# High-by-high matmuls first in steps 0 and 1, the second tile's scores in four quadrants, the first third in a new order

## The chip, the cores and the metric

The kernel runs on one core of a Trainium2 chip. Its time is the device time of one execution in microseconds (us); lower is better. Five engines work in parallel, each through its own list of instructions in order: PE (TensorE, matmuls), ACT (ScalarE), DVE (VectorE), POOL (GpSimd) and SP (SyncE, which here issues most transfers).

## The reference

Attention in chunks of 64 tokens, then a feed-forward layer with g = h·cos(h):

```
scores = scale * q_c @ k_c^T        # batch 8, heads 8, 9 chunks of 64, head size 64
attn   = softmax(scores); out = attn @ v_c
x = out as 4608 tokens x 512
h = x @ w_in                        # 512 x 2048
g = h * cos(h)
result = g @ w_out                  # 2048 x 512
```

The inputs are float32, or arrive as 8-byte words that the kernel turns into float32 itself (here they do, for the weights).

## The kernel before, in words

The 4608 tokens are nine tiles of 512. For a tile, a pair of heads (hp 0 to 3) is one 128x512 array: its scores are 16 matmuls of 64x64 on PE, DVE takes each chunk row's maximum from them and subtracts it, ACT takes the exponential, DVE sums and inverts, DVE or POOL divides, PE transposes (tiles 0 and 1) into a tile `pts`, and PE multiplies with the values. The result x is needed as two parts: `x_hi` (a rounding cast by ACT) and `x_lo` (the remainder, by DVE). Every weight is treated the same way: ACT decodes two halves of its words, DVE joins them, ACT or DVE casts `w_hi`, DVE or POOL makes `w_lo`. A product of two such operands is three matmuls: high by high, high by low, low by high.

The feed-forward layer runs in steps s; a step takes one block of 128 of the 2048 columns. `hidden` (L701) makes h for the step: 12 matmuls of 128x512, three for each of four column blocks cc of x (cc is the head pair hp). Then comes a chain of six: ACT (turn count), DVE, ACT (sine), DVE (the product g), a cast `g_hi` and a remainder `g_lo`. `project` (L735) multiplies with w_out: three matmuls for each of four banks `acc`, 12 in a step, three steps behind. Two banks `h` are in turns, so that `hidden` of step s waits until step s-2 has its g.

The program builds its work as a list of pieces (`piece`, L1079): an engine, an estimated length, a function that records the instructions, and the pieces that it waits for. Which piece comes when on which engine is read from two tables, `RANK` and `ELSEWHERE` (L91 on), whose numbers were made ahead; `in_order` (L282) only sorts by them. What each engine runs is then fixed.

Tile 0's and tile 1's attention is in `early` (L1144). In both, a head pair's scores fill one bank: head 0's into partitions 0 to 63, head 1's into 64 to 127 (`scores_early`, L489), so that the 16 matmuls alternate between two quadrants of the array (rows of head 0 with columns of head 0, rows of head 1 with columns of head 1). Tile 1's four head pairs use the banks a0 and a1 in turns. From tile 2 on, `scores` (L522) makes two head pairs at once into both banks, one bank for each head, and a bank's upper and lower partitions take the even and odd chunks: four quadrants in turn, 64 matmuls in the trace's count for two head pairs (a matmul of float32 there counts twice). Steps 0 and 1 (s < `BY_HEAD`, L1287) record their hidden matmuls in four pieces each, one for each cc with its three matmuls; a piece waits for all of the weight's split, w_lo included (`split`), and both halves of its x, x_lo included (`x_done`).

Of the kernel before, what the change touches and what calls it, by code (L numbers as in the profile page):

```python
# [288 lines left out]
def attention_then_cos_ffn(ctx: ExitStack, tc, qT, kT, v, w_in, w_out, out, wide):  # L289
# [232 lines left out]
    def scores(t, g, banks):  # L522
# [3 lines left out]
        for j in range(2):  # L526
            qt, kt = queries.pop((t, 2 * g + j))
            for c in range(NCH):
                pr, par = divmod(c, 2)
                cs, ps = slice(c * CH, (c + 1) * CH), slice(par * CH, (par + 1) * CH)  # L530
                o = (j * NPR + pr) * CH
                for h in range(2):
                    hs = slice(h * CH, (h + 1) * CH)

# [1964 lines left out]
```

## Time and profile before

| what | us |
|---|---|
| median of three runs | 775.62 |
| lowest and highest of the three | 774.85 and 776.1 |
| span of the profiled execution, first to last instruction | 773.5 |
| PE busy in it | 762.5 (99%) |
| DVE busy in it | 644.4 (83%) |
| ACT busy in it | 444.8 (58%) |

No other time of the profiled execution is given than its span. An engine's busy share is its busy time by the span. PE is busy nearly always, so what counts is where it still waits, and how many matmuls it has to run; in the rows on PE, matmuls overlap, and the start of a row to the start of the next says what a row costs.

### The profile page before, as it was taken

To read this page: it belongs to the slowest core of one execution; us is meant where nothing else is said; L and a number is where in the kernel's file an instruction comes from. 1 tells how busy PE (TensorE), PEld (TensorE's weight loads), DVE (VectorE), ACT (ScalarE), POOL (GpSimd) and SP (SyncE) were. 2 spreads that over 40 slices of the span, in tenths; PEclk is the share of its full clock that TensorE was granted. 3 is DMA by queue.
4 is the path that set the end of the run, shared out by engine and by line. 5 is a ranking of instruction groups with operands and counts; after the bars stand their busy time and mean duration, and the time that the engine had idled before them with its cause. 6 is when DMAs were issued, how large, how long until landed. Compare 5 with 4: busy or idle time off the path is not lost.

```text
span 773.5 us, 16085 instructions
## 1 busy us (share of the span) xinstructions
PE 762.5 (99%) x6100; PEld 676.3 (87%) x6100; DVE 644.4 (83%) x1112; ACT 444.8 (58%) x818; POOL 267.1 (35%) x245
## 2 busy tenths in 40 slices
PE   7999999999999999999999999999999999999997
PEld 6888888888999988888888888888888888989997
DVE  5998989989899889897898868785998577798874
ACT  5999876456874456554553435546554355557651
POOL 3422133776542444246222321200202315265231
PEclk9999999999999999999999999999999999999999
DMA  9995600579979753777974545587535567988983
GB/s 341 401 410 197 205 2 1 190 263 382 320 255 310 243 165 108 226 259 243 326 265 140 174 135 188 181 290 242 179 104 180 158 208 229 294 300 284 361 305 103
DMA packets 95757, 177.22 MB, mean 229 GB/s; under 512 B 9152, under 2 KB 39872, under 8 KB 95680
## 3 DMA queue, kind: packets, MB, share of 16 engines
q1 hardware_dynamic: 95104, 175.15, 66.2%
q8 instruction: 48, 0.79, 0.4%
q10 hardware_dynamic: 576, 1.05, 0.4%
q14 instruction: 29, 0.24, 0.1%
HBM read 127.93 MB, written 48.23 MB: 228 GB/s over the span
## 4 chain that ended last, share of the span: by engine, by line
PE 84%; DVE 8%; DMA 4%; ACT 2%; issue 1%; SPq 0%; DVEq 0%; ACTq 0%
PE acc L323 39%; PE h L323 33%; PE a L323 12%; DMA w_in<-sums 2%; DMA sums<-qt 1%; DMA combo<-w_in 1%; DVE w_in L970 1%; DMA kt<-in_kT_dram 1%; DVE z L595 0%; DVE w_in L344 0%; DVE pts L640 0%; DVE w_in L937 0%; DVE g L724 0%; DVE m L546 0%; DVE g L726 0%
## 5 line engine op out<-in xcount | busy, mean ns | idle before, releaser
L323 PE MATMUL acc<-w_out,g_hi 128*128 128x512 f32 (+1 forms) x976 | 278.1, 369 | 0.0
L323 PE MATMUL h<-x,w_in 128*128 128x512 f32 (+1 forms) x960 | 226.4, 364 | 0.1
L323 PEld LDWEIGHTS acc<-w_out,g_hi 128*128 128x128 f32 x976 | 178.5, 189 | 22.9
L323 PEld LDWEIGHTS h<-x,w_in 128*128 128x128 f32 x960 | 171.1, 189 | 22.7 <-ACT g_hi L340 0.4
L323 PE MATMUL acc<-w_out,g_lo 128*128 128x512 f32 (+1 forms) x488 | 179.2, 367 | 0.0
L344 POOL TENSOR_TENSOR g_lo<-g,g_hi 128x512 fp32r<-128x512 f32 x30 | 41.4, 1380 | 194.3 <-ACT g_hi L340 70.9
L323 PEld LDWEIGHTS acc<-w_out,g_lo 128*128 128x128 f32 x488 | 92.4, 189 | 11.8 <-DVE g_lo L344 0.2
L323 PE MATMUL h<-w_in,w_in 128*128 128x512 f32 (+1 forms) x384 | 98.3, 354 | 0.8 <-DVE w_in L970 0.7
L323 PEld LDWEIGHTS h<-w_in,w_in 128*128 128x128 f32 x384 | 65.6, 190 | 9.7 <-DVE w_in L970 2.0
L980 ACT ACTIVATE w_in<-w_in 128x512 f32<-128x512 f32 x64 | 39.3, 628 | 17.8 <-DVE w_in L976 17.7
L344 DVE TENSOR_TENSOR g_lo<-g,g_hi 128x512 fp32r<-128x512 f32 x59 | 44.1, 747 | 4.0 <-ACT g_hi L340 2.2
L340 ACT CAST g_hi<-g 128x512 fp32r<-128x512 f32 x48 | 29.7, 618 | 27.8 <-PE acc L323 14.5
L323 PE MATMUL a<-w_in,w_in 128*128 128x512 f32 (+1 forms) x204 | 42.5, 348 | 0.0
L323 PE MATMUL a<-x,w_in 128*128 128x512 f32 (+1 forms) x192 | 41.2, 353 | 0.0
L344 POOL TENSOR_TENSOR g_lo<-w_in,g_hi 128x512 fp32r<-128x512 f32 x12 | 18.9, 1577 | 64.3 <-ACT g_hi L340 42.6
L323 PEld LDWEIGHTS a<-w_in,w_in 128*128 128x128 f32 x204 | 34.5, 190 | 4.0
L323 PEld LDWEIGHTS a<-x,w_in 128*128 128x128 f32 x192 | 33.2, 190 | 4.1
L967 ACT COPY a<-h 128x512 f32<-128x512 f32 x28 | 16.0, 571 | 32.3 <-PE h L323 32.1
L723 ACT ACTIVATE g<-h 128x512 int32<-128x512 f32 x32 | 19.3, 602 | 26.1 <-PE h L323 26.0
L973 ACT ACTIVATE w_in<-h 128x512 int32<-128x512 f32 x32 | 19.1, 597 | 26.3 <-PE h L323 24.7
L976 DVE SCALAR_TENSOR_TENSOR w_in<-w_in,h 128x512 f32<-128x512 int32 x32 | 21.9, 685 | 12.6 <-ACT w_in L973 11.8
L344 DVE TENSOR_TENSOR g_lo<-w_in,g_hi 128x512 fp32r<-128x512 f32 x34 | 28.8, 855 | 3.8 <-ACT g_hi L340 3.2
(294 smaller groups left out, 1509.6 us busy)
## 6 DMA issues: line engine op xcount, KB each, us to landing
w_in<-combo SPq DMA_DIRECT2D x84, 512.0 KB, 4.8
combo<-w_in SPq DMA_DIRECT2D x56, 256.0 KB, 4.5
w_in<-combo SPq DMA_DIRECT2D x56, 256.0 KB, 5.3
qt<-in_qT_dram SPq DMA_DIRECT2D x36, 256.0 KB, 5.6
w_in<-in_w_in_dram SPq DMA_DIRECT2D x16, 512.0 KB, 9.7
kt<-in_kT_dram SPq DMA_DIRECT2D x32, 256.0 KB, 5.6
w_out<-in_w_out_dram SPq DMA_DIRECT2D x16, 512.0 KB, 9.9
gathered<-w_in SPq DMA_DIRECT2D x32, 256.0 KB, 3.7
```

What stands on the lines that cost most here:

```text
L323: kept(nc.tensor.matmul(*args, **kw))
L340: kept(nc.scalar.copy(out=out, in_=in_))
L344: kept(eng.tensor_tensor(out, a, b, op=op))
L723: lambda: kept(nc.scalar.activation(n, h, AF.Identity, bias=0.25, scale=0.5 / math.pi)),
L967: kept(nc.scalar.copy(out=out, in_=in_))
L970: kept(nc.vector.tensor_tensor(out, a, b, op=ALU.add))
L973: kept(nc.scalar.activation(g.bitcast(I32), h, AF.Identity, bias=0.25, scale=0.5 / math.pi))
L976: kept(nc.vector.scalar_tensor_tensor(g, g.bitcast(I32), -2.0 * math.pi, h, op0=ALU.mult, op1=ALU.add))
L980: kept(nc.scalar.activation(g, g, AF.Sin, bias=0.5 * math.pi))
```

## The change

Four things change.

1. In steps 0 and 1, `hidden` records the four high-by-high matmuls as pieces of their own, which need only `w_hi` and `x_hi`. The two with a low part form a second piece for each cc.
2. Tile 1's scores are made by `scores`, two head pairs at once into banks a0 and a1, in four quadrants. A chunk c = 2 pr + par of tile 1 goes to the partitions of pr mod 2, so that chunks 0 and 1 lie in the lower half, 2 and 3 in the upper. Four pieces for scores become two. The weights' layout and the transposed tile's column index follow.
3. `RANK` and `ELSEWHERE` hold new numbers, which change the order in the first third of the work. Behind some 1,220 of PE's 3,158 rows the order is the same as before.
4. With the order, single operations change engine: the copies of transposed tiles and some casts from ACT to DVE, some remainders to POOL.

```diff
@@ scores @@
-                cs, ps = slice(c * CH, (c + 1) * CH), slice(par * CH, (par + 1) * CH)
-                o = (j * NPR + pr) * CH
+                row, at = (pr % 2, pr - pr % 2 + par) if t == 1 else (par, pr)
+                cs, ps = slice(c * CH, (c + 1) * CH), slice(row * CH, (row + 1) * CH)
+                o = (j * NPR + at) * CH
...
-        e = weights_of(t, g).rearrange("p a (r h) k -> p a r h k", h=2)
+        e = weights_of(t, g).rearrange("p a (h r) k -> p a r h k" if t == 1 else "p a (r h) k -> p a r h k", h=2)
@@ weighted @@
+                        at = 4 * h + pr if t == 1 else 2 * pr + h
                         matmul(
-                            banks[par][hs, o : o + CH], vt[ks, fs], pts[ks, fs],
+                            banks[par][hs, o : o + CH], vt[ks, fs], pts[ks, at * CH : (at + 1) * CH],
@@ hidden @@
-    def hidden(t, fc, ccs=range(4), h=None):
+    def hidden(t, fc, ccs=range(4), h=None, highs=True, lows=True):
...
-            matmul(h, w_hi[:, ws], x_hi, start=(cc == 0), stop=False)
+            if not lows:
+                matmul(h, w_hi[:, ws], x_hi, start=(cc == 0), stop=False)
+                continue
+            if highs:
+                matmul(h, w_hi[:, ws], x_hi, start=(cc == 0), stop=False)
             matmul(h, w_hi[:, ws], x_lo, start=False, stop=False)
             matmul(h, w_lo[:, ws], x_hi, start=False, stop=(cc == NCC - 1))
@@ early @@
-        for hp in range(HP):
-            which = ("a", hp % 2) if t else ("acc", hp)
+        for g in range(2) if t else ():
+            key = ("s", t, g)
+            now = piece(
+                PE, 1.1, made_by(key, lambda g=g: scores(t, g, (bank("a", 0), bank("a", 1)))),
+                banks_free.get(("a", 0)), banks_free.get(("a", 1)), at=max(here["qk", t, 2 * g + j] for j in range(2)),
+                lag=0.35, pairs=64,
+            )
+            below = []
+            for h in range(2):
+                m = piece(DVE, 0.6, rest_of(key, 2 * h), now)
+                below.append(piece(DVE, 0.6, rest_of(key, 2 * h + 1), m, turned_out.get((t - 1, g))))
+                banks_free["a", h] = below[-1]
...
@@ steps 0 and 1 @@
         if s < BY_HEAD:
-            for cc in range(NCC):
-                def go(t=t, fc=fc, key=key, cc=cc):
-                    made[key] = hidden(t, fc, (cc,), made.get(key))
-                stream = piece(
-                    PE, 0.648, go, stream if cc else begun, split["in", fc], bank_at, *x_done[t][2 * cc : 2 * cc + 2],
-                    pairs=3, main=True,
-                )
-                begun = begun if cc else stream
+            for lows in (False, True):
+                for cc in range(NCC):
+                    def go(t=t, fc=fc, key=key, cc=cc, lows=lows):
+                        made[key] = hidden(t, fc, (cc,), made.get(key), not lows, lows)
+                    stream = piece(
+                        PE, 0.432 if lows else 0.216, go, stream if cc or lows else begun,
+                        split["in", fc] if lows else high_of["in", fc], bank_at,
+                        *(x_done if lows else x_high)[t][2 * cc : 2 * cc + 2], pairs=2 if lows else 1, main=True,
+                    )
+                    begun = begun if cc or lows else stream
```

The order on PE around the end of steps 0 and 1, before. Names: `w_in_479` and `w_in_525` are the split weights of steps 0 and 1, `w_in_569` of step 2; `x_0` and `x_2` are the high parts of tile 0's x for cc 0 and 1 and for cc 2 and 3, `x_1` and `x_3` the low parts; `a<-kt,qt` are tile 1's scores, a row of 16 for one head pair (its first head pair's stands far ahead, among tile 0's transposes).

```order
L323 MATMUL h<-x_2_516,w_in_479 128x512
L323 MATMUL h<-x_0_442,w_in_525 128x512
L323 MATMUL h<-x_1_443,w_in_525 128x512
L323 MATMUL h<-x_0_442,w_in_525 128x512
L323 MATMUL a_584<-kt,qt 64x64 x16
L323 MATMUL h<-x_2_516,w_in_525 128x512
L323 MATMUL h<-x_3_517,w_in_525 128x512
L323 MATMUL h<-x_2_516,w_in_525 128x512 x2
L323 MATMUL h<-x_3_517,w_in_525 128x512
L323 MATMUL h<-x_2_516,w_in_525 128x512
L323 MATMUL a_618<-kt,qt 64x64 x16
L323 MATMUL a_642<-kt,qt 64x64 x16
```

The same place in the change, in two pieces. Here `w_in_459` and `w_in_522` are the weights of steps 0 and 1, `x_0_422` and `x_2_496` the high parts of x; two of step 0's high-by-high matmuls (cc 0 and 1) stand ahead of the first row.

```order
L323 MATMUL h<-x_0_422,w_in_522 128x512 x2
L323 MATMUL h<-x_2_496,w_in_459 128x512 x2
L323 MATMUL h<-x_1_423,w_in_459 128x512
L323 MATMUL h<-x_0_422,w_in_459 128x512
L323 MATMUL h<-x_1_423,w_in_459 128x512
L323 MATMUL h<-x_0_422,w_in_459 128x512
L323 MATMUL h<-x_2_496,w_in_522 128x512 x2
L323 MATMUL h<-x_1_423,w_in_522 128x512
L323 MATMUL h<-x_0_422,w_in_522 128x512
L323 MATMUL h<-x_3_497,w_in_459 128x512
```

Ten more matmuls down the list the first group of scores (`a_570`, `a_571`) has run, and then stands:

```order
L323 MATMUL a_570<-kt,qt 64x64
L323 MATMUL a_571<-kt,qt 64x64
L323 MATMUL h<-x_3_497,w_in_522 128x512
L323 MATMUL h<-x_2_496,w_in_522 128x512
L323 MATMUL a_625<-kt,qt 64x64
L323 MATMUL a_626<-kt,qt 64x64
```

The high-by-high matmuls of both steps moved to the front; the scores of tile 1 moved behind nearly all of steps 0 and 1, and the second group (`a_625`, `a_626`, the same two banks) stands two matmuls behind the first, ahead of step 2.

DVE at the scores of tile 1, in the change (L547 is the maximum, L551 the subtraction, which is the last to read a bank; L730 and L732 belong to step 0's g):

```order
L730 SCALAR_TENSOR_TENSOR g<-g,h 128x512 [waits Activation_49]
L338 CAST w_in_609<-w 128x512 [waits DMAHW2_49,DVE_49]
L338 CAST w_out_611<-w 128x512 [waits DMAHW3_49,DVE_49]
L547 TENSOR_REDUCE m<-a_570 128x8 [waits PE_49]
L547 TENSOR_REDUCE m<-a_571 128x8 [waits PE_49]
L551 TENSOR_TENSOR e_604<-a_571,m 128x2x256 [waits DVE_49]
L551 TENSOR_TENSOR e_604<-a_570,m 128x2x256
L732 TENSOR_TENSOR g<-h,g 128x512 [waits Activation_49]
```

Before, a maximum and a subtraction for a single head pair stood between other work; now the four for two head pairs are in one run.

ACT at steps 0 and 1, in the change (L731 is the sine, L580 the exponential; each change from one to the other has a table load):

```order
L731 ACT_TABLE_LOAD
L731 ACTIVATE g<-g 128x512
L403 ACTIVATE w<-w_in_99 128x512
L729 ACTIVATE g<-h 128x512
L403 ACTIVATE w<-w_out_94 128x512
L580 ACT_TABLE_LOAD
L580 ACTIVATE e_604<-e_604 128x512 x2
L731 ACT_TABLE_LOAD
L731 ACTIVATE g<-g 128x512
```

Before, no exponential stood between the sines of steps 0 and 1, and tile 1's four came behind one another later. From step 0's sine to the first sine behind tile 1's last exponential ACT loads three tables before, and five now.

## Rows read from the trace of the kernel before

**Rows 1.** The page's first part: busy time of each engine
```profile
PE 762.5 (99%) x6100; PEld 676.3 (87%) x6100; DVE 644.4 (83%) x1112; ACT 444.8 (58%) x818; POOL 267.1 (35%) x245
```
**Rows 2.** Busy us by stretch: PE, weight loads, DVE, ACT, POOL, clock, DMA, GB/s
```profile
15.00:20.00 5.00, 3.53 (x108) 2.78 (x107) 4.96 (x13) 5.00 (x12) 4.13 (x3) 1.00 1.04 408
20.00:30.00 10.00, 10.00 (x162) 8.26 (x155) 9.55 (x19) 9.83 (x18) 3.85 (x3) 1.00 1.04 397
...
300.00:400.00 100.00, 99.30 (x707) 85.97 (x698) 88.17 (x151) 56.23 (x91) 38.61 (x34) 1.00 0.75 251
400.00:700.00 300.00, 299.93 (x2046) 263.83 (x2045) 238.63 (x407) 148.14 (x252) 76.73 (x68) 1.00 0.62 203
```
**Rows 3.** PE in order of time, 20 to 55 us: start, length, instructions
```profile
20.88 0.69 PE L323 MATMUL acc<-pts,x 64*64 64x64 f32 x32
21.51 3.50 PE L323 MATMUL h<-x,w_in 128*128 128x512 f32 x15
...
27.51 2.08 PE L323 MATMUL a<-kt,qt 64*64 64x64 f32 x64
29.52 2.86 PE L323 MATMUL h<-x,w_in 128*128 128x512 f32 x12
...
34.81 2.75 PE L323 MATMUL h<-x,w_in 128*128 128x512 f32 x12
37.40 0.59 PE L323 MATMUL acc<-w_out,g_hi 128*128 128x512 f32 x2
...
53.60 0.38 PE L323 MATMUL acc<-w_out,g_lo 128*128 128x512 f32 x1
54.07 1.16 PE L323 MATMUL a<-pts,vt 64*64 64x64 f32 x64
```
**Rows 4.** PE in order of time at the third tile's scores
```profile
106.22 1.16 PE L323 MATMUL a<-kt,qt 64*64 64x64 f32 x64
107.31 2.86 PE L323 MATMUL h<-x,w_in 128*128 128x512 f32 x12
```
**Rows 5.** DVE in order of time, the opening and at 34 us
```profile
8.74 0.69 DVE L503 TENSOR_REDUCE m<-acc 128x8 f32<-128x512 f32 x1 [0.81 <-PE acc L323]
9.47 0.69 DVE L507 TENSOR_TENSOR e<-acc,m 128x512 f32<-128x512 f32 x1
10.54 0.17 DVE L599 TENSOR_SCALAR z<-z 128x8 f32<-128x8 f32 x1 [0.38 <-ACT e L515]
...
20.29 0.42 DVE L338 CAST w_in<-w 128x512 fp32r<-128x512 f32 x1
...
34.05 1.28 DVE L503 TENSOR_REDUCE m<-a 128x8 f32<-128x512 f32 x2
```
**Rows 6.** ACT in order of time, 18 to 29 us
```profile
18.56 0.70 ACT L685 CAST x<-acc 128x256 fp32r<-128x256 f32 x2
...
20.71 0.77 ACT L403 ACTIVATE w<-w_in 128x512 f32<-128x512 f32 x1
...
22.90 0.91 ACT L403 ACTIVATE w<-w_in 128x512 f32<-128x512 f32 x1
23.67 0.92 ACT L405 ACTIVATE half<-w_out 128x512 uint32<-128x512 uint32 x1
24.44 0.64 ACT L723 ACTIVATE g<-h 128x512 int32<-128x512 f32 x1
...
26.24 1.28 ACT L725 ACT_TABLE_LOAD   x1
27.54 0.63 ACT L725 ACTIVATE g<-g 128x512 f32<-128x512 f32 x1
28.07 0.67 ACT L403 ACTIVATE w<-w_in 128x512 f32<-128x512 f32 x1
```
**Rows 7.** POOL in order of time: step 0's w_in remainder
```profile
18.09 1.81 POOL L344 TENSOR_TENSOR w_in<-w,w_in 128x512 fp32r<-128x512 f32 x1
```
**Rows 8.** PE's waits over the span: line, what for, us in total, times, longest
```profile
PE h L323 <- DVE w_in L970: 0.7, 2, 0.4
```

More of the change, by code (lines that the diff above doesn't have):

```diff
@@ L1126, in attention_then_cos_ffn @@
     joined = {}
+    high_of = {}
     turn_of = sorted(due, key=lambda b: (due[b], b))
@@ L1135, in attention_then_cos_ffn @@
         joined[name, fc] = piece(DVE, 0.6, rest_of(key, 2), u, l, port=True)
-        h = piece(ACT, 0.52, rest_of(key, 3), joined[name, fc], other=(DVE, 0.45, True))
+        h = high_of[name, fc] = piece(ACT, 0.52, rest_of(key, 3), joined[name, fc], other=(DVE, 0.45, True))
         split[name, fc] = piece(DVE, 0.6, rest_of(key, 4), h, port=True, other=(POOL, 1.25, False))
     x_done = {}
+    x_high = {}
     banks_free = {}
@@ L1146, in early @@
         more_values = None
-        for hp in range(HP):
-            which = ("a", hp % 2) if t else ("acc", hp)
+        for g in range(2) if t else ():
[10 more added lines that the diff above has]
+                banks_free["a", h] = below[-1]
+            for hp in (2 * g, 2 * g + 1):
+                e[hp] = piece(ACT, 0.6, lambda hp=hp: exponentials_early(t, hp), *below, table=AF.Exp)
+        for hp in () if t else range(HP):
+            which = "acc", hp
             key = ("s", t, hp)
@@ L1154, in early @@
             m = piece(DVE, 0.6, rest_of(key, 0), s[hp])
-            room = turned_out.get((t - 1, hp // 2))
-            if t == 0 and hp in BY_CHUNK:
+            if hp in BY_CHUNK:
                 m = piece(DVE, 0.25, rest_of(key, 2), m, port=True)
@@ L1159, in early @@
                 continue
-            banks_free[which] = piece(DVE, 0.6, rest_of(key, 1), m, room)
+            banks_free[which] = piece(DVE, 0.6, rest_of(key, 1), m)
             e[hp] = piece(ACT, 0.6, lambda hp=hp: exponentials_early(t, hp), banks_free[which], table=AF.Exp)
@@ L1203, in early @@
                 x_done.setdefault(t, []).append(banks_free[which[i // 2]])
+                x_high.setdefault(t, []).append(hi)
         return w
```

368 rows, old and new, of tables (ELSEWHERE, RANK) are left out of this document.

## The prediction

> **What bounds the kernel now.** I read the busy times first. PE is busy for 762.5 of 773.5 us [rows 1], so a gain must take matmuls away or let PE start earlier; no other engine is near that. The table by stretch shows where this holds [rows 2]: from 20 us on PE has no idle time worth the name (10.00 of 10.00, and 299.93 of 300 late in the run). Only in the opening, up to 20 us, does PE wait (3.53 of 5.00), and there DVE (4.96) and ACT (5.00) are the full ones. They stay nearly full behind it (9.55 and 9.83 of 10), under a PE that is full as well. PE's own list then shows the joint [rows 3]: the last values product of tile 0 starts at 20.88, steps 0 and 1 run from 21.51, the last two head pairs of tile 1's scores start at 27.51, and step 2 starts at 29.52. **Behind that row both programs have the same matmuls left**, and before runs them without idle time. So the question is when the changed kernel starts step 2, and what waits come or go behind it.
>
> **The change, step by step.** Sums are made against the profiled span of 773.5; the median of the runs is 775.6, and I carry the 2.1 between them as a constant.
>
> *What it saves on PE.* Two head pairs of scores cost 29.52 - 27.51 = 2.0 us before [rows 3]. In four quadrants, at the third tile, they cost 107.31 - 106.22 = 1.09 [rows 4]. For four head pairs that is 4.0 against 2.2, but before ran one of them in an idle gap of the opening. The new sequence isn't the third tile's: chunks 0 and 1 go to the same half, so a quadrant comes again after two matmuls, not after four. No row shows that sequence. Its ends are 1.09 (four quadrants at work) and 2.0 (two), for each group. I take 1.09, the nearer row: while the second pair of matmuls of one chunk half runs, the first pair of the other can.
>
> *Opening: the last values product.* DVE sets it. Before, DVE runs without a gap from 10.54 to the end of the cast of step 1's w_hi at 20.71 [rows 5]: 10.2 us. In the change the same stretch loses one maximum and one subtraction of tile 1 and gains two copies of `pts`, all about 0.60 apart, so its length stays. It can start 0.5 earlier: the third maximum comes straight behind the first subtraction, at 9.47 + 0.60 = 10.07. Allowing 0.4 for copies that wait for their transposes, the cast ends at 20.65. The last copy of `pts` stands two operations ahead of it (a join of about 0.6 and the cast of 0.42) and ends near 19.8. The last values product then runs from 19.9 to 20.6, 1.0 ahead of before (20.88) [rows 3].
>
> *Steps 0 and 1.* Their high-by-high matmuls need the casts of x_hi alone. ACT's last four of these stand behind the decoding of the third weight, which needs a buffer that POOL frees with step 0's w_lo. Before, POOL starts that at 18.09 and takes 1.81 [rows 7]; in the change it starts at 18.0. So ACT decodes from 19.85 (0.77) and casts from 20.6, 0.33 apart (two start 0.70 for the pair) [rows 6]: done at 21.9. If POOL were quicker, the values product would still hold the casts to 21.4. By 21.9 PE has run the four high-by-high matmuls of cc 0 and 1, out of 24. Of the other 20, 18 stand ahead of the first group of scores. A matmul costs 0.216 (twelve from 34.81 to 37.40 [rows 3]). 18 x 0.216 = 3.9, so the first group starts at 25.8 and ends at **26.9**. Before, the same work (24 matmuls and two head pairs) is done at 27.51. Here the change is 0.6 ahead.
>
> *Where it gives that back.* The second group writes the same two banks and needs both subtractions behind the first. On DVE that is a maximum, a maximum, a subtraction that waits for them, and another: 0.60 + 0.60 + 0.73 (from 8.74 to 9.47, where one waits for the other) + 0.69 [rows 5]; the pair at 34.05 takes 1.28. Together 2.6 us from 26.95, which is also when DVE comes free: step 0's h ends near 24.9, ACT's turn count takes 0.64 [rows 6], then stand DVE's next of 0.6 to 0.7 and two casts of 0.42. So the banks are free at 29.55. PE has two matmuls (0.43) for the wait and stands 2.2 us. Nothing else is ready in its list: step 2 stands behind the second group, and it needs step 0's g out of its bank, which DVE makes only behind the subtractions, near 30.1. The second group runs from 29.55 to 30.65, and **step 2 starts at 30.65 against 29.52: +1.1 us**.
>
> *Behind it.* The two extra table loads cost ACT 2 x 1.28 = 2.6, and they stand ahead of step 1's sine, which step 3 needs. ACT from step 0's turn count at 24.95 to that sine: two turn counts (0.5 each), four decodings at 0.77 (22.90 to 23.67 to 24.44), three table loads at 1.30 (26.24 to 27.54), four sines or exponentials at 0.53 (27.54 to 28.07) [rows 6]: 10.1, so 35.1, and DVE's product 0.75 behind it, 35.85. PE is through step 2 and the first projection at 30.65 + 2 x 2.59 plus fill, 35.95; before it starts step 3 at 34.81 [rows 3]. That fits by 0.1, so I count nothing. Further on, copies and splits that PE needs come 0.5 us or more ahead. Two things come back: the values product of tile 1 waits 0.25 before (53.60 + 0.216 to 54.07), and in the change its copies are done some 2 us ahead. Of other waits behind the first third, 0.7 on DVE [rows 8], I let none go, since what they wait for comes from PE too and moves with it. Transfers: SP issues the loads of weights and heads in the same order, and each has landed by the time of its use before, which is no later than now.
>
> *A rule against it.* Table switches: the rows show 1.28 us for the load, and the next activation 1.30 after the load's start, with the instruction ahead of it ending at the load [rows 6]. The Trainium skill, "ScalarE: Activation LUTs", section "What ACT_TABLE_LOAD costs", gives some 1.28 us for the load and 1.38 more for a drain, 2.66 for every switch; the trace agrees with the load and has no drain. By the page the two extra loads alone would be 5.3 us of ACT.
>
> **Sum.** +1.1 for the start of step 2, -0.25 for the wait that goes, +0.15 for the tie on ACT: **+1.0**. The span becomes 774.5 and the time 776.6.
>
> **Rivals.** A measurement of this kernel can tell about 0.2%, 1.55 us, from no change; so my forecast is "no difference", on the slow side (below 777.2).
>
> 1. *The quadrants don't overlap* (slower). The place is tile 1's two groups of scores. If a quadrant that comes again after two matmuls holds the next ones, a group costs 2.0 instead of 1.09: +0.9 twice, total +2.8, 778.4. It decides from a price of about 1.4 a group. For it: no row has this sequence. Against: the two pairs of a half have different quadrants from the next half's. Chance 0.13.
> 2. *ACT becomes the bound of step 3* (slower). The thirteen operations above fit by 0.1. If the decodings take their full 0.9, as their rows say, instead of 0.77 apart, or a remainder on POOL comes late, ACT slips by 0.5 to 1.5 and PE with it: +1.5 to +2.5, 777.1 to 778.1. For it: ACT is full here before [rows 2], with two loads fewer. Against: the spacing is read in just such a full stretch. Chance 0.19.
> 3. *The opening pays and the later waits go* (faster). If the casts end at 21.4 and the first group of scores at 26.4, step 2 starts at 30.15, +0.6. A new order that also took away what PE still waits later, the 0.25 above, the 0.4 of [rows 8] and the 0.7 between 300 and 400 [rows 2], would end at -0.75. It needs 0.8 more, from subtractions of the first group that DVE gets done while PE is still at steps 0 and 1; then it is 773.9 or less. For it: the order is new over a third of the run. Against: behind 20 us there is hardly any idle time to win [rows 2]. Chance 0.08.
> 4. *A drain at every switch.* Three loads stand between the sines of steps 0 and 1, with 1.38 more for each: step 3 4 us later, total +5, 780.6. That is the page's rule; the rows above exclude it so far. Chance 0.02.
>
> **How the numbers follow.** 0.58 is left for my forecast, between 774.5 and 777.2. Faster by over 0.2% is rival 3 (0.08); slower is rivals 1, 2 and 4 (0.34); same is the rest. The range has its low end at 774.8: the forecast with the quicker casts (-0.5), the runs' own spread (774.85 to 776.1) and a part of the later waits. Its high end, 778.6, takes in rivals 1 and 2.
>
> **What would show it.** In the changed profile: the last values product of tile 0 near 19.9; 18 matmuls without a gap from 21.9; the first group of scores 1.1 long, ending near 26.9; then a wait of PE of about 2.2 us for DVE's subtraction, the largest behind the opening; step 2 near 30.65 and step 3 near 36; five table loads in ACT's first 75 us behind step 0, each 1.3 long; from 36 us on PE as full as before. The prediction is wrong if step 2 starts before 29.5 or after 31.5, if a group of scores takes 2 us, or if PE has a wait of more than 0.5 us anywhere from 36 to 260.

## The result, and the profile after

The changed kernel takes **782.04 us** (median of 4 runs, 781.60 to 782.26) where before takes 775.52 in the same comparison (774.85 to 776.10): a ratio of **1.0083**, 95% interval 1.0069 to 1.0098. It is 6.5 us slower. The profiled execution spans 780.2 us, before's 773.5.

The busy line answers to [rows 1]. PE is busy 1.9 us longer with the same 6,100 matmuls, and the rest of the 6.7 us is idle time.

```profile
PE 764.4 (98%) x6100; PEld 675.5 (87%) x6100; DVE 646.2 (83%) x1118; ACT 447.0 (57%) x816; POOL 267.3 (34%) x243
```

The table by stretch, columns as in [rows 2], with a finer one of a single microsecond behind it:

```profile
15.00:20.00 5.00, 4.06 (x109) 2.92 (x107) 4.78 (x12) 4.57 (x11) 3.62 (x3) 1.00 1.03 405
20.00:30.00 10.00, 7.72 (x134) 5.96 (x133) 9.68 (x20) 9.49 (x17) 4.17 (x3) 1.00 1.04 397
30.00:35.00 5.00, 5.00 (x75) 4.35 (x70) 4.62 (x10) 4.81 (x6) 2.12 (x2) 0.66 1.03 407
...
31.00:32.00 1.00, 1.00 (x23) 0.88 (x17) 0.69 (x2) 0.99 (x2) 1.00 (x1) 0.50 1.04 416
```

Two things are new here. PE is idle for 2.3 of the 10 us from 20 to 30, where before had none. And the granted clock, 1.00 all through before, is 0.66 from 30 to 35 and 0.50 in the microsecond from 31: the lower of its two levels. PE's list in order of time, where [rows 3] had the same place:

```profile
20.22 0.69 PE L323 MATMUL acc<-pts,x 64*64 64x64 f32 x32 [0.16 <-DVE pts L338]
20.84 5.08 PE L323 MATMUL h<-x,w_in 128*128 128x512 f32 x21
25.85 1.21 PE L323 MATMUL a<-kt,qt 64*64 64x64 f32 x64
26.99 0.70 PE L323 MATMUL h<-x,w_in 128*128 128x512 f32 x2
29.81 1.82 PE L323 MATMUL a<-kt,qt 64*64 64x64 f32 x64 [2.12 <-issue]
31.55 3.84 PE L323 MATMUL h<-x,w_in 128*128 128x512 f32 x12
35.23 0.59 PE L323 MATMUL acc<-w_out,g_hi 128*128 128x512 f32 x2
```

The first group of scores takes 26.99 - 25.85 = 1.14 us. PE then waits 2.12 us for the second group's banks. That group takes 31.55 - 29.81 = 1.74, with the same 64 matmuls, and step 2 takes 35.23 - 31.55 = 3.68, where twelve such matmuls took 2.59 before [rows 3]. These two are the work at the lower clock: (1.74 - 1.14) + (3.68 - 2.59) = 1.7 us.

The other new rows of PE lie far behind the opening (the engine's list again; the bracket is the wait and what ended it):

```profile
181.76 0.48 PE L323 MATMUL acc<-w_out,g_lo 128*128 128x512 f32 x1 [1.18 <-DVE g_lo L344]
...
203.99 0.48 PE L323 MATMUL acc<-w_out,g_lo 128*128 128x512 f32 x1 [0.73 <-DVE g_lo L344]
```

Before has no wait over 0.25 us on PE between 36 and 290.

To follow the loss along the run I number PE's matmuls and take, for the n-th, how much later it starts than before's n-th, less the same at n = 50, so that the landing of the first loads, which differs by up to 1.3 us between executions, drops out (added matmuls aren't counted). The columns are before's times of those matmuls. Between orders that differ, 0.6 us either way at 155 us is only the order of PE's own list.

```
us into before            91    155    214    266    415    644   ratio of times, 95% interval
the change              2.44   3.12   5.51   6.05   6.23   6.20   1.0083  1.0069 to 1.0098
e0_change               2.59   3.28   5.67   6.42   7.41   7.38   1.0071  1.0057 to 1.0086
e1_fill                 0.75   1.47   3.94   4.41   4.32   4.29   1.0072  1.0059 to 1.0085
e2_opening_only         3.44   3.44   3.43   3.43   2.84   2.81   1.0032  1.0019 to 1.0044
e3_later_only           0.10   0.78   3.25   4.79   5.64   5.65   1.0063  1.0049 to 1.0076
e4_fill_opening_only    2.20   2.19   2.21   2.21   1.59   1.56   1.0034  1.0021 to 1.0046
e5_three_back           1.11   1.82   3.22   3.91   5.04   5.01   1.0068  1.0053 to 1.0083
e6_engines_back         1.14   5.44   9.16  11.70  13.78  13.78   1.0203  1.0186 to 1.0220
e7_half_fill            2.06   2.77   5.16   5.60   6.06   6.03   1.0052  1.0039 to 1.0064
e8_four_back            2.92   3.60   4.39   6.05   7.02   7.02   1.0081  1.0063 to 1.0099
e9_quadrants_undone     0.96   1.65   4.16   4.62   5.55   5.54   1.0068  1.0047 to 1.0088
e10_highs_with_lows     2.78   3.50   5.90   6.35   6.03   6.00   1.0084  1.0064 to 1.0104
e11_fill_four_back      2.63   3.31   4.09   5.87   5.79   5.80   1.0050  1.0033 to 1.0067
e12_late_from_150       0.06   0.66   3.20   3.66   4.42   4.39   1.0059  1.0045 to 1.0073
e13_late_70_to_150      0.06   0.18   0.17   0.18  -0.03  -0.06   0.9999  0.9990 to 1.0007
e14_late_from_200      -0.04  -0.04  -0.32   0.06   0.82   0.79   1.0011  1.0001 to 1.0020
e15_first_pair_early    1.02   1.73   4.14   4.65   5.07   5.04   1.0068  1.0056 to 1.0081
e16_only_150_to_200     0.09   0.69   2.16   2.16   1.68   1.65   1.0014  1.0005 to 1.0023
e17_order_only          0.27   0.87   3.89   4.01   3.41   3.50   1.0041  1.0027 to 1.0055
```

(The last row is e17_order_without_engines.) The change loses 2.4 us by 91 us, another 3.1 by 214, and 0.7 behind that. The change and e0_change are the same program, and their two executions differ by 1.2 us at 644, nearly all of it made between 214 and 415. So behind 214 us a difference of less than that between two rows says little by itself.

### The profile page after: what moved, and what is told of

The parts are those of the page before. It is cut to its first block, busy times and chain, and to the rows that moved or that the text cites. A ratio compares the mean times of both kernels' runs of the same rounds, so it can differ in the third digit from the quotient of the medians.

```text
span 780.2 us, 16084 instructions
## 1 busy us (share of the span) xinstructions
PE 764.4 (98%) x6100; PEld 675.5 (87%) x6100; DVE 646.2 (83%) x1118; ACT 447.0 (57%) x816; POOL 267.3 (34%) x243
## 4 chain that ended last, share of the span: by engine, by line
PE 85%; DVE 8%; DMA 4%; issue 1%; ACT 1%; POOL 1%; SPq 0%; DVEq 0%; POOLq 0%
PE acc L323 39%; PE h L323 33%; PE a L323 12%; DMA w_in<-sums 1%; DMA diffs<-w_in 1%; DMA sums<-qt 1%; DVE g_lo L344 1%; DVE pts L641 1%; DMA x<-diffs 1%; DVE w_in L344 1%; DMA kt<-in_kT_dram 1%; DVE w L344 0%; POOL w_in L344 0%; PE a L615 0%; DVE pts L637 0%
## 5 line engine op out<-in xcount | busy, mean ns | idle before, releaser
L344 POOL TENSOR_TENSOR g_lo<-g,g_hi 128x512 fp32r<-128x512 f32 x27 | 36.0, 1334 | 145.2 <-DVE g_hi L338 54.9
L340 ACT CAST g_hi<-g 128x512 fp32r<-128x512 f32 x55 | 34.0, 617 | 31.7 <-PE acc L323 14.0
L344 DVE TENSOR_TENSOR g_lo<-g,g_hi 128x512 fp32r<-128x512 f32 x62 | 47.5, 766 | 5.2 <-ACT g_hi L340 3.6
L986 ACT ACTIVATE g<-g 128x512 f32<-128x512 f32 x40 | 25.0, 626 | 13.4 <-DVE g L982 13.3
L344 POOL TENSOR_TENSOR e<-e,z 128x512 f32<-128x512 f32 x16 | 17.8, 1120 | 41.9 <-ACT g_hi L340 16.4
```

The source lines that it names most:

```text
L340: kept(nc.scalar.copy(out=out, in_=in_))
L344: kept(eng.tensor_tensor(out, a, b, op=op))
L986: kept(nc.scalar.activation(g, g, AF.Sin, bias=0.5 * math.pi))
```

## The experiments

Theory: the loss has three parts, the opening as forecast (about 1 us), the lower clock behind PE's wait (about 1.7), and new waits that the later order brings (3 to 4). Rivals: the slow second group has another cause than the clock; the later waits are only the lateness of the opening handed on. In the experiments' rows a line number is 36 or 37 lower than in the change, since their tables take fewer lines.

### e0_change: the change once more

No edit; it is there to stand beside e5 to e7 on one chip.

> The change itself once more, so that the runs beside it are compared on one chip: 6.5 us over before by the first comparison, with PE's waits of 2.1 us ahead of the second group of scores, 1.2 at 182 us and 0.7 at 204 us, and a stretch of some 3.4 us at the lower clock behind the first of them.

Measured: 780.69 us against 775.22, and every part as before, with the clock at 0.50 from 30 to 33 us. The total is 1 us less than in the first comparison, with intervals that overlap; so differences under 1 us aren't read below between kernels that weren't timed side by side.

### e1_fill, e7_half_fill: work in PE's wait

```diff
     for i, by in in_order(work, RANK, ELSEWHERE):
         work[i][2](*([by] if work[i][8] else []))
+        if i == 281:
+            b = bank("acc", 0)
+            for _ in range(17):
+                kept(nc.tensor.transpose(out=b[:, :P], in_=ident, identity=ident))
```

(8 in e7_half_fill; piece 281 is the last pair of step 1's matmuls.)

> The change, with 17 transposes of the identity (about 2.3 us, of 128x128, into a bank that nobody reads; they compute nothing that is used) on PE between the last two matmuls of step 1 and the second group of tile 1's scores, where PE stood idle for 2.1 us. Theory clock: the idle time made the granted clock fall to 0.5 for 3.4 us; with PE busy there it stays at 1.00, the second group takes 1.1 us instead of 1.74 and step 2 2.6 to 2.7 instead of 3.68: 1.6 us less than the change, 780.4. Rival (the slower second group and step 2 have another cause, contention with DVE's or DMA's work): the group and step 2 stay at 1.7 and 3.7, and the time stays at 782.0 or rises by the fill's excess of 0.2.

> The change with 8 unused transposes (1 us) in PE's idle time behind step 1 in place of 17: about 1.1 us of it stays idle. If the clock falls for a wait of about 1 us as it did for 2.1, the second group and step 2 stay at 1.7 and 3.7 us and the time is that of the change; if not, they take 1.1 and 2.7, and the time is that of the full fill, about 1.6 us under the change of the same call (0.9 by the two calls so far).

PE's list of e1_fill at the same place:

```profile
26.46 2.02 PE L2436 MATMUL acc<-ident 128*128 128x128 f32 x17
28.74 1.21 PE L287 MATMUL a<-kt,qt 64*64 64x64 f32 x64 [0.26 <-PE acc L2436]
29.88 2.86 PE L287 MATMUL h<-x,w_in 128*128 128x512 f32 x12
32.58 0.59 PE L287 MATMUL acc<-w_out,g_hi 128*128 128x512 f32 x2
```

With PE at work in the gap the clock stays at 1.00, the second group takes 1.14 and step 2 takes 2.70, and the lag at 91 us is 0.75 instead of 2.44. Theory clock holds in the trace. In time the gain is less plain. e1_fill is at 1.0072, no different from e0_change, which was timed elsewhere; e7_half_fill, timed beside e0_change, is 1.8 us under it. The trace of e7_half_fill holds a surprise: no fall behind the gap, half of which was still idle, but one at 15 to 20 us (granted 0.68), with a lag of 2.06. **The fall isn't tied to one gap.**

### e9_quadrants_undone: without the quadrants

```diff
-        for g in range(2) if t else ():
-            key = ("s", t, g)
-            now = piece(
-                PE, 1.1, made_by(key, lambda g=g: scores(t, g, (bank("a", 0), bank("a", 1)))),
...
+        for hp in range(HP):
+            which = ("a", hp % 2) if t else ("acc", hp)
             key = ("s", t, hp)
```

> The change with the scores of tile 1 as before made them, one head pair after the other, in the change's order otherwise (four pieces of about 1.04 us on PE in the places of two of 1.1). Theory waiting: the quadrants took 2 us of PE's time out of a place where PE waits for DVE anyway. Without them PE works where it stood, its wait of 2.1 us goes to 0.3 or less, step 2 starts within 0.3 us of where it starts in the change, and the clock stays at 1.00 behind 25 us: the same time as executions of the change without the fall of the clock, 1.6 us under those with it; 779 to 780. Rival (the quadrants save time): step 2 starts 1.5 to 2 us later than in the change, and the time is 782 or more.

```profile
24.57 2.08 PE L287 MATMUL a<-kt,qt 64*64 64x64 f32 x64
...
27.32 1.15 PE L287 MATMUL a<-kt,qt 64*64 64x64 f32 x32
28.64 1.15 PE L287 MATMUL a<-kt,qt 64*64 64x64 f32 x32 [0.17 <-PE a L287]
29.71 2.86 PE L287 MATMUL h<-x,w_in 128*128 128x512 f32 x12
```

The same place in e5_three_back, whose opening is that of the change, quadrants and all, and whose profiled execution had no fall of the clock:

```profile
19.59 5.06 PE L287 MATMUL h<-x,w_in 128*128 128x512 f32 x21
24.59 1.21 PE L287 MATMUL a<-kt,qt 64*64 64x64 f32 x64
...
28.55 1.21 PE L287 MATMUL a<-kt,qt 64*64 64x64 f32 x64 [2.12 <-issue]
29.69 2.86 PE L287 MATMUL h<-x,w_in 128*128 128x512 f32 x12
...
34.97 1.24 PE L287 MATMUL h<-x,w_in 128*128 128x512 f32 x5
```

The scores begin at 24.57 and 24.59, step 2 at 29.71 and 29.69. Four head pairs cost PE 4.2 us in one and 2.3 in the other, and it makes no difference: what the quadrants save, PE waits. Without them PE is busy, and the clock stayed at 1.00 in this execution; the mean granted clock of the six timed runs was 1.00 in four, where e0_change's six had 0.997 to 0.999 (a fall behind PE's last matmul counts in these means too, so they only hint). The time is 779.62 us, as expected by theory waiting.

### e10_highs_with_lows, e15_first_pair_early: the rest of the opening

```diff
-RANK: the high-by-high matmuls of steps 0 and 1 ahead
+RANK: each in front of the two with low parts of its cc
```

> The change with the eight high-by-high matmuls of steps 0 and 1 put back in front of those with low parts, cc by cc. Theory: they were never waiting for low parts behind 21 us, and only the first of them fills idle time ahead of it (0.2 us); the first group of scores starts 0 to 0.4 us later, and the time is the change's within what can be measured. Rival (the split is what makes the opening work): PE waits for low parts among the triples, the group of scores starts 1 us later or more.

From the second values product of tile 0 to the first group of scores it is 24.78 - 18.79 = 5.99 us, where the change has 25.85 - 20.22 = 5.63: 0.36 later. The time, 1.0084, is the change's. The wait doesn't take this up: the second group starts 28.74 - 18.79 = 9.95 us behind the same product, where the change has 29.81 - 20.22 = 9.59, again 0.36 later. So the split of the steps by itself is worth a third of a microsecond, too little to show in the time.

```diff
 e9_quadrants_undone
-RANK: the first head pair's scores behind steps 0 and 1
+RANK: they, their maximum, subtraction and exponential where before has them
```

> The change with the quadrants undone (as e9), and the scores of tile 1's first head pair, their maximum, subtraction and exponential, back where before has them, among tile 0's transposes at 12 us, where PE waits anyway. Theory idle place: what the opening loses without the fall of the clock, 1.0 us in the traces, is these 1.05 us of scores moved from PE's idle time into its busy stretch; step 2 starts 0.8 to 1.2 us earlier than in e9, the clock stays at 1.00 and the time is 0.8 to 1.0 under e9's, 3.5 to 5 over before because of the later order. Rival: step 2 is bound by DVE and ACT (step 0's sine); it starts within 0.3 us of e9's, and the time stays.

```profile
29.26 2.86 PE L287 MATMUL h<-x,w_in 128*128 128x512 f32 x12
...
34.92 1.35 PE L287 MATMUL h<-x,w_in 128*128 128x512 f32 x5 [0.22 <-DVE g L696]
```

Step 2 starts 0.45 us earlier than in e9, half of what was expected, and then step 3 waits for g; at 91 us the lag is 1.02, e9's 0.96. Neither expectation has the right start of step 2, but the rival's outcome holds: the time stays (1.0068, as e9), and the opening's own loss of 1 us isn't the place of these scores. With PE's part taken out, step 3 waits for DVE's g.

### e2, e3, e4: the opening or the later order

```diff
 e2_opening_only, and e4_fill_opening_only with e1's fill
-RANK, ELSEWHERE: the change's
+RANK, ELSEWHERE: the change's up to step 8 (70 us), before's from there on
 e3_later_only
-RANK, ELSEWHERE: before's
+RANK, ELSEWHERE: before's up to step 8, the change's from there on
```

> The change's code and its order up to step 8 (some 70 us), then the order of before and its choice of engines. Theory order: the waits at 165, 182 and 204 us come from the new order of the stretch behind 70 us, so only the opening's loss is left, 2.7 us in the profiles: 778.2. Rival lateness: the opening being 2.7 us later makes the waits (DMA and DVE fall out of step): 782, with PE's waits of 0.7 to 1.2 us between 155 and 215 us still there.

> The code of before and its order up to step 8 (some 70 us), then the order of the change and its choice of engines. Theory order: the later order by itself costs 3.3 us at 150 to 215 us and up to 4 in all: 778.8 to 779.5, with waits of PE on DVE's casts of g between 155 and 215 us. Rival lateness: without the late opening the order costs nothing, 775.5 give or take 0.5.

> Both: the 17 unused transposes in PE's idle time behind step 1, and the order of before from step 8 on. Theory clock and order together: what was forecast blind is left, before plus 1.0 to 1.3: 776.5 to 776.9. Rivals: 778.2 if the clock is not the cause of the slow second group, 780.4 if the late order is not the cause of the later waits.

With before's order behind 70 us PE has no wait over 0.21 us up to 290, although the opening is as late as in the change; with the change's order behind an opening that isn't late, the waits of 0.24, 1.18 and 0.81 us at 162, 178 and 201 us are there. Lateness falls as a cause. e3 measures the later order: 779.41 us, 4.8 over before by the medians. e2 (777.18) and e4 (777.13) came out alike. In the traces e4 gains 1.25 on e2, in the medians nothing; e4's five runs reach from 775.85 to 778.46, with mean clocks from 1.00 down to 0.995, so in some of them the clock probably fell elsewhere. Its two runs at 1.00 took 775.85 and 776.41. Both kernels lose 1 us more where the two orders are joined, at 70 us: e2's lag at 91 us is 3.44 against 2.44.

### e5, e6, e8, e11: work back on its engine

Why is `g_lo` late at 181? DVE's list in the change:

```profile
173.80 1.29 DVE L344 TENSOR_TENSOR w<-w_in 128x512 f32<-128x512 f32 x2
...
177.09 0.95 DVE L338 CAST g_hi<-g 128x512 fp32r<-128x512 f32 x1
177.96 1.22 DVE L933 TENSOR_TENSOR pts<-e 128x512 f32<-128x512 f32 x1
179.10 1.21 DVE L933 TENSOR_TENSOR vt<-e,e 128x512 f32<-128x512 f32 x1
...
181.03 0.68 DVE L344 TENSOR_TENSOR g_lo<-g,g_hi 128x512 fp32r<-128x512 f32 x1
```

and in before, where the reassembly of that strip (`w<-w_in`) is POOL's, at 167.37:

```profile
172.88 0.68 DVE L344 TENSOR_TENSOR g_lo<-g,g_hi 128x512 fp32r<-128x512 f32 x1
173.48 0.68 DVE L927 TENSOR_TENSOR pts<-e 128x512 f32<-128x512 f32 x1
174.09 0.68 DVE L927 TENSOR_TENSOR vt<-e,e 128x512 f32<-128x512 f32 x1
```

In the change DVE has the strip as well, and the low part that PE waits for stands behind two differences instead of in front of them. Three of the change's rows are also long: 0.95, 1.22 and 1.21 us, where a cast at 180.35 takes 0.43 and the two differences before take 0.68 each. POOL is at work beside them (from 176.13, for 3.63 us). That is 1.6 us more, which alone exceeds PE's wait; no run takes only this work away.

```diff
 e5_three_back
-ELSEWHERE
+ELSEWHERE with 639, 718 and 719 (to POOL)
 e8_four_back, and e11_fill_four_back with e1's fill
-ELSEWHERE
+ELSEWHERE with 639, 718 and 719, without 759 (back to DVE)
 e6_engines_back
-ELSEWHERE
+ELSEWHERE: before's engine for each piece from step 8 on
```

> The change with three pieces of work given back from DVE to POOL, as before had them, in the order of the change: the sixth block's reassembly and its sums (3.3 us of DVE's time at 174 to 177 us) and step 28's low part of g, which PE waits for at 181.76. Theory engines: DVE's list there is what makes PE wait, so the wait of 1.18 us goes and the time falls by 1.0 to 1.4 us under the change of the same call. Rival order: the low part is late because of its place behind other work, on POOL behind 3.6 us of remainders; PE waits as long or longer, and the time stays within 0.3 us or rises by up to 1.

> The three pieces given back as in e5, and a fourth swapped: the reassembly of two strips that POOL does at 200.5 us in the change (2.8 us, while two of DVE's 128x8 operations take 0.8 and 1.2 us) goes back to DVE, as before had it. Theory contention: DVE's small operations and step 31's low part of g are late because POOL works at the same time; PE's wait at 200 to 204 us falls from 0.8 to 0.2 or less and the time is 0.5 to 0.8 under e5's, by the traces. Rival: the low part is late because it stands behind the maxima of the next tile; the wait stays at 0.6 to 0.9, or moves a little.

> e8 with the 17 unused transposes in PE's idle time as well: what both repairs give together. If clock and engines are independent: e8 less 1.6 us where e8's executions had the fall of the clock; 776.5 to 778.5 on a chip where before takes 775. Rival: the wait shows up elsewhere again, 779 or more.

> The change's order all through, but from step 8 on (some 70 us) each piece on the engine that it had before: some 100 pieces differ. Theory engines: the waits of 0.2 to 1.2 us between 155 and 260 us come from work that moved to DVE, and go with it: 3 to 4 us under the change of the same call, 2.7 over before. Rival order: an order that was planned for other engines waits elsewhere; the time stays within 1 us of the change or rises.

Of e5's three pieces, 718 and 719 are the strip's reassembly and its sums. 639 is not the low part that PE waits for at 181.76, as the expectation has it, but the next step's, which DVE makes at 185.41.

In e5 the wait of 1.18 is gone, and from 155 to 214 us the lag grows by 1.40 instead of 2.39, as theory engines had it. In e8 the one at 204 is gone too (growth 0.79). But the gain doesn't reach the end. e8's list of PE has a new row:

```profile
258.04 1.58 PE L287 MATMUL h<-w_in,w_in 128*128 128x256 f32 x12 [0.98 <-DMA w_in<-combo]
```

The change starts the same matmuls at 258.46, without a wait: PE comes earlier in e8 and waits for the strip's load. In e11 they wait 1.10 us at 256.87, for a cast of DVE. From 155 to 415 us the change's lag grows by 3.11, e5's by 3.22, e8's by 3.42, and the times say the same (780.17 and 781.44). e11 is 2.6 us under e8, timed side by side, but its profiled execution had the clock at 0.50 from 15 to 20 us, and its lag of 2.63 at 91 us is no better than the change's. The expectation of 776.5 to 778.5 missed: 778.84. And e6 shows that engines and order belong together: with before's engines under the change's order six waits of 0.8 us or more appear between 100 and 300, the longest of 1.63, and the time is 790.61. My theory engines falls as an account of the total.

### e12, e13, e14, e16, e17: which stretch

```diff
-RANK, ELSEWHERE: before's
+e12: the change's from step 24 on (151 us)
+e13: the change's between step 8 and step 24
+e14: the change's from some 200 us on
+e16: the change's between 151 and 200 us
+e17: as e16, the order alone, each piece on before's engine
```

> The code of before, its order and engines up to step 24 (some 151 us), then the change's. If the loss comes from the change's order behind 150 us (what DVE has ahead of each cast of g, and when the strips for the next stage are written and loaded): 3.5 to 5 us over before, as with the change's order from 70 us on. If the order of 70 to 150 us sets up the later waits: less than 1.5 over before.

> The code of before and its order, but the pieces that it has between step 8 and step 24 (some 66 to 151 us) in the change's order and on the change's engines. If the loss comes from behind 150 us: within 0.7 us of before, PE without a wait over 0.2 us up to 290. If it comes from here: 3 us over before or more.

> The code of before, its order and engines up to some 200 us, then the change's. If the loss is that of 160 to 205 us (PE's waits for g there): within 1 us of before. If it is what follows (strips written and loaded later, waits at 256 to 330 us): 2 to 3 us over before.

> The code of before and its order, but the 189 pieces that it has between 151 and some 200 us in the change's order and, for 16 of them, on the change's engines. Theory: the loss is made here; 3 to 4 us over before, with PE's waits of 1.2 to 1.5 us for g's low part near 178 us and 0.7 to 1.1 near 200, and none behind them that before doesn't have. Rival: the stretch costs only together with what follows; under 1.5 us over before.

> As e16, with every piece on before's engine: the new order of the same stretch alone. If the 16 pieces on other engines make the loss, it goes to under 1 us over before; if the order does, it stays at 3 us or more, or rises, as it did when all later engines went back.

The new order of 70 to 150 us costs nothing (0.9999), though it moves 297 of the table's places. From 151 on it costs 0.59%, nearly all of e3's 0.63%. The two halves alone cost 0.14% and 0.11%: e16's expectation of 3 to 4 us was wrong, its rival right. e12's list of PE shows what comes only when both are there:

```profile
177.74 0.48 PE L286 MATMUL acc<-w_out,g_lo 128*128 128x512 f32 x1 [1.45 <-DVE g_lo L307]
...
200.35 0.48 PE L286 MATMUL acc<-w_out,g_lo 128*128 128x512 f32 x1 [1.07 <-DVE g_lo L307]
```

e16 has the first of these (1.45) and not the second, e14 neither. By the lags of these single executions e12's 4.4 us are 2.1 from the stretch of 150 to 200 as in e16, 1.0 at the second wait, and 1.2 between 214 and 415 as in e14 (1.1), where strips are written and loaded later. e17 ends the theory of engines: the same order with before's engines is worse, 1.0041 against 1.0014.

DVE's lists show why the second wait needs both halves. First e12, then e16:

```profile
195.75 1.28 DVE L509 TENSOR_REDUCE m<-a 128x8 f32<-128x512 f32 x2
197.06 1.08 DVE L516 TENSOR_SCALAR m<-m 128x8 f32<-128x8 f32 x1
198.06 1.57 DVE L307 TENSOR_TENSOR w_in<-half,w_in 128x256 fp32r<-128x256 f32 x1
```

```profile
195.70 1.28 DVE L509 TENSOR_REDUCE m<-a 128x8 f32<-128x512 f32 x2
196.89 0.42 DVE L307 TENSOR_TENSOR w_in<-half,w_in 128x256 fp32r<-128x256 f32 x1
197.22 0.17 DVE L516 TENSOR_SCALAR m<-m 128x8 f32<-128x8 f32 x1
```

DVE comes to this place at the same time in both. The later half of the table gives the next strip's reassembly to POOL, which does it here in e12 (from 196.84, for 2.50 us); in e16 DVE does it, at 200.23. Beside POOL's work two small operations take 1.08 and 1.57 us instead of 0.17 and 0.42, and `g_lo` starts at 199.62 instead of 197.30. e14 has POOL's work too (from 195.46), but before's list, in which `g_lo` starts at 195.90 and PE doesn't wait. e8, which gives that strip back to DVE, has lost the wait in the same way.

## Why the prediction was wrong

Forecast: 776.6 us, no difference. Measured: 782.04. By its steps:

**What it saves on PE** held: 1.14 us for a group against 1.09 taken, so rival 1 is out. **Opening** and **Steps 0 and 1** held within 0.25 us, once the 0.28 is taken off by which the first scores already start later in this execution: values product 19.94 (19.9 forecast), first group 25.57 to 26.71 (25.8 to 26.9). **Where it gives that back** held in its walk: DVE's two maxima and two subtractions,

```profile
27.09 1.29 DVE L547 TENSOR_REDUCE m<-a 128x8 f32<-128x512 f32 x2
28.41 1.29 DVE L551 TENSOR_TENSOR e<-a,m 128x512 f32<-128x512 f32 x2
```

are the 2.6 us forecast, and PE's wait is 2.12 for 2.2. One remark of the forecast was off without an effect: the 0.6 by which the change is ahead at 26.9 counts 24 matmuls, where 22 have run, so it is 0.2; the start of step 2 doesn't rest on it. The step failed in its last line, the price of what follows the wait. The second group was put at 1.09 and step 2 at 2.59, at full clock, and they took 1.74 and 3.68. In e5, where the clock stayed up, step 2 starts 29.69 - 19.59 = 10.10 us behind steps 0 and 1 and step 3 another 5.28 later; by the forecast's own numbers (20.6 to 30.65 and 35.95) it was 10.05 and 5.30. So the term was +1.1 as forecast **plus 1.7** for the clock, which the text didn't name: all through before the granted clock is 1.00, so no row gave a price for 1.2 GHz, but before has no wait of PE over 0.4 us behind 20 us either [rows 8]. A wait five times as long had no row, and should have been bounded by the same matmuls at the lower level. The Trainium skill, "TensorE: Matmul & The Clock Gate", section "What's actually happening", says that a PE which hasn't been busy runs at 1.2 GHz until it has been; the change's trace agrees, with 0.50 granted from 31 to 33 us behind the wait, while e5 and e6 keep 1.00 behind the same wait. That would have been a rival of its own.

How sure is it that it falls? Of seven profiled executions with this gap (the change, e0, e2, e5, e6, e8, e10) five have the fall behind it. Their lag at 91 us is 2.4 to 2.9 (e2, with the 1 us more of its joint, aside), that of e5 and e6 without the fall 1.1. None of the seven with before's opening (before, e3, e12, e13, e14, e16, e17) has a fall ahead of PE's last matmuls.

**Behind it** failed on the larger part. ACT's tie held: what follows each of its three table loads starts 1.29 to 1.30 us behind the load's start, without a drain, and in e5 step 3 follows step 2 as forecast, so rivals 2 and 4 are out. (The 0.15 that the sum adds for this tie has no step in the forecast's text, which counts nothing for it; the runs show none either.)

```profile
26.93 1.28 ACT L731 ACT_TABLE_LOAD   x1
28.22 0.63 ACT L731 ACTIVATE g<-g 128x512 f32<-128x512 f32 x1
...
30.48 1.28 ACT L580 ACT_TABLE_LOAD   x1
...
32.95 1.28 ACT L731 ACT_TABLE_LOAD   x1
```

The 0.25 booked as gain came too: between 40 and 70 us the lag falls by 0.29 in the change and by 0.30 in e1_fill. What failed is the sentence that behind 36 us copies and splits "come 0.5 us or more ahead". The new order reaches through 1,220 of PE's 3,158 rows, and I walked only its first 36 us. e3 and e12 measure what I left at zero: 4.9 and 4.6 us by their ratios, made between 150 and 415 us. The change's trace shows most of its part at two low parts of g, one behind a strip's reassembly on DVE, the other made late by one on POOL. But e8 loses both waits and isn't faster, so how the loss behind 150 us divides stays open. The prediction's own test, a wait over 0.5 us between 36 and 260, names the place: there are two.

Rival 3 had the sign wrong (and its terms, -0.75 and -0.8 from 775.6, end at 774.05, not 773.9): of the new order it asked only whether old waits could go. The rival that was missing is its mirror, that a new order brings waits of its own where PE had none to lose; in a stretch where PE is at 10.00 of 10.00 every wait is a loss.

The sum as it came out, by the lags: 2.4 by 91 us (1.1 as forecast, 1.7 from the clock, less 0.3 for the wait that went), 3.1 by 214, 0.7 later: 6.2, with 0.28 from the start, of 6.7 in span. Without the fall of the clock, in e5, it is 1.1 by 91 us, near the +1.0 that was forecast for the whole run.

No version here beats before; of the change's parts none gained more than the third of a microsecond of e10, and e13, the only one of its stretches that costs nothing, is before within 0.1%.

## What to carry to other kernels

Time saved on the busiest engine in front of a wait is not saved, and can cost: first find what the next instruction of its list waits for, and price the work behind a long idle stretch at the lower clock as well as at the full one. When a table reorders a third of the program, compare each engine's list at the few places where the full engine takes another's result with least slack, all the way to where the orders meet, not only around the edit. Look also at what POOL does beside DVE at that moment, not only at each engine's own list. And a repair is measured at the end of the run: in e8 two waits went away at 182 and 204 us, a new one for a transfer came at 258, and the time was no better.

## What the runs showed of the hardware

The granted clock fell behind a wait of 1.9 to 2.1 us in five of seven executions, and in two others of the same opening, e7 and e11, at 15 to 20 us, behind a stretch in which PE was busy for less of the time than before (the tables by stretch of e11 and of before):

```profile
5.00:15.00 10.00, 7.05 (x166) 5.84 (x161) 8.20 (x19) 6.68 (x25) 3.13 (x3) 0.97 1.04 398
15.00:20.00 5.00, 4.62 (x68) 3.40 (x71) 3.49 (x9) 3.25 (x8) 2.60 (x2) 0.50 1.02 400
```

```profile
5.00:15.00 10.00, 8.74 (x173) 8.14 (x174) 6.57 (x16) 5.25 (x22) 2.09 (x2) 1.00 1.04 392
```

e5 had 6.84 of 10 there, e9 7.08, and no fall, so busy time alone doesn't tell; what decides it in one execution is open.

POOL's work can slow DVE's, as e12 and e16 show above. In the change two operations of DVE on 128x8 elements take 0.82 and 1.24 us while POOL reassembles two strips (200.54, 2.77 us); with that work taken off POOL, in e8, they take 0.17 and 0.16:

```profile
201.03 0.82 DVE L554 TENSOR_SCALAR m<-m 128x8 f32<-128x8 f32 x1
...
202.10 1.24 DVE L554 TENSOR_SCALAR m<-m 128x8 f32<-128x8 f32 x1
```

```profile
200.01 0.17 DVE L518 TENSOR_SCALAR m<-m 128x8 f32<-128x8 f32 x1
...
200.43 0.16 DVE L518 TENSOR_SCALAR m<-m 128x8 f32<-128x8 f32 x1
```

The Trainium skill, "SBUF — State Buffer", section "Who interferes with whom", says that the two share one pair of ports, which, where both need it, one of them holds for a whole instruction; the rows agree, with up to 1.1 us for an operation of 0.16.
